# Half-array products for x and logits, decay by diagonal products, and routing steps spread over more iterations, in a three-stage kernel

## Chip, core and metric

One core of a Trainium2 chip runs the whole program. The metric is the device time of one execution in microseconds (us). Five engines work side by side and wait for each other through semaphores: TensorE (PE, matrix products, with its weight loads shown as PEld), VectorE (DVE), ScalarE (ACT), GpSimd (POOL) and SyncE (SP, which here only issues transfers). Each engine takes its instructions in the order of its own queue.

## What is computed

Three stages, each feeding the next, all in float32:

```python
# attention with a decaying state, B=4, H=8, S=768, D=48
for t in range(S):
    cur = einsum('bhd,bhe->bhde', u[None] * kt, vt)
    y[:, :, t] = einsum('bhd,bhde->bhe', rt, state + cur)
    state = w[None, :, :, None] * state + einsum('bhd,bhe->bhde', kt, vt)
x = y.transpose(0, 2, 1, 3).reshape(B * S, H * D)          # 3072 x 384
# mixture of 8 experts, one chosen per token, 384 -> 1024 -> 384
logits = x @ w_gate; e = argmax(logits)
out = softmax(logits)[e] * sigmoid(x @ w_output_gate)[e] * (relu(x @ w1[e]) @ w2[e])
# dense feed-forward, 384 -> 1536 -> 384
result = (silu(out @ w_gate2) * (out @ w_val)) @ w_out
```

## The kernel before, in words

**The attention** takes the 3072 tokens in 24 tiles of 128, six to each of the four sequences. Heads lie in four pairs (q), two of 48 channels padded to 64 in each (j), so that a pair fills the 128 partitions. A loop of 27 iterations (`for i in range(NTILE + 3)`) is written out by hand: inside `tc.manual_schedule`, PE, DVE, ACT and POOL issue in program order. Iteration i holds, in this order, work for several tiles:

- `scaled_r(i+1)`: the tile `rdT` on DVE (L384), and loads of later tiles on SP.
- `bonus(i+1)`: a sum `cb` on DVE (L396) and eight multiplies of the identity into `dsb` on ACT (L400).
- `scores(i)`: 8 products `pss` on PE (L410), each two instructions, with a 64x128 stationary operand; two masked copies into `dsb` on DVE (L414). The two `pss` buffers are the two of the pool `ps_s`.
- the second half of `emit` for tile i-3: a transpose of the logits `lT` on PE (`psl`, L126), and their sum over the four pairs, `lg`, on DVE (L127).
- `state(i-1)`: 8 products `pskv` on PE (L432); at a batch's first tile a copy on DVE (L437), at the following four one multiply-add per pair on DVE (L442), state times decay plus product; at its last tile nothing.
- `scaled_k(i+2)`: `ck`, `kdT` and `kdc` on POOL (L373 to L377).
- `outputs(i-1)`: products `psy` on PE, from the state (L459) and from `dsb` (L466), and the copy `yT` on ACT (L471).
- the first half of `emit` for tile i-2: logits `psl` (L114) and four transposes `psx` (L120) on PE, the copies `lT` (L116) and `xt` (L122) on ACT, and the store of x by SP (L123).

**Routing.** When a batch's last `lg` is there, a generator `route` (and for the first three batches `gate`, for the third also `head_tokens`) is put into the list `routing`. Each call of `advance` takes one step from it, one or two small DVE instructions; the calls stand between the other work of the loop. Before a step on PE the generator yields `TENSOR`; such a step is taken only by `advance(TENSOR)`, and not until two ticks of a counter `now` (three ticks per iteration) have passed since the step before it:

```python
if kind != tensor or kind and since > now[0] - 2:
    return
```

`scores` calls `advance` four times, `state` two to eight times (more from tile HURRY = 18 on), and three calls stand between. The step `psw` (L210) on PE needs the selections made on DVE (L199 to L206).

**Way out of the attention.** `head_tokens` (L495) turns the third batch's routing into row numbers `rows_h`; two gathers on POOL (L1029) fetch tokens for the first expert, `moe.transposed` transposes them on PE (`pt`, L1043) at the start of iteration 24, and `moe.head` begins the first expert's products (`pha`, L1074) after iteration 26, with the fourth batch's routing handed out between its steps.

**PSUM** has eight banks: `ps_m` three (warm-up, `psl`, `pskv`), `ps_s` two, `ps_y` two (`psy`, `psx`), `ps_r` one (routing). From about 150 us on follow the experts, with the third stage's weights converted beside them, and the third stage; they are bound to the order of their own loops.

## Time and profile before

| | us |
|---|---|
| median of 3 runs (856.60 to 857.57) | 857.28 |
| profiled execution, its time | 855.75 |
| its span, first to last instruction | 854.0 |
| PE busy in the span | 820.0 |
| DVE busy | 534.2 |
| ACT busy | 350.9 |
| POOL busy | 215.7 |

Busy time is that in which an engine runs instructions; PE's is modelled at its end, so that a busy PE is not PE at its peak. The granted clock is the share of 2.4 GHz that TensorE was given, with two levels, 1.2 and 2.4 GHz. In a timeline a row merges instructions of one line that follow each other; the time in brackets behind a row is idle time before it and what ended it.

### The profile page before, as it was taken

The page shows a single profiled execution, that of the slowest core. Times are in us where ns is not written, and L with a number is a line of the kernel's source. Part 1 is how long each engine was busy: PE and PEld are TensorE (multiplying, and loading weights), DVE is VectorE, ACT ScalarE, POOL GpSimd, SP SyncE. Part 2 cuts the span into 40 slices and gives each one's busy share as a digit, 9 for nine tenths or more (in the row PEclk, how much of TensorE's full clock was granted, in tenths as well). Part 3 has the DMA queues.
Part 4 walks back from the last instruction along what each step waited for, and adds up shares of the span by engine and source line. Part 5 has one row for each costly group of instructions (what it writes and reads, how often), then busy time and mean ns, then how long its engine had stood idle before and what let it go on. Part 6 is the DMA issues. An engine that isn't in the chain of part 4 may idle for free.

```text
span 854.0 us, 14581 instructions
## 1 busy us (share of the span) xinstructions
PE 820.0 (96%) x5535; PEld 736.6 (86%) x5536; DVE 534.2 (63%) x1097; ACT 350.9 (41%) x793; POOL 215.7 (25%) x206
## 2 busy tenths in 40 slices
PE   7997889999999999999999999999999999999994
PEld 4776677998999989998888888888888888899994
DVE  7889997789999989973555334333533533244532
ACT  3875565474565665663433212221221222122321
POOL 7998672444424422200000100100010010001000
PEclk8999989999999999999999999999999999999997
DMA  8897864665887877442220100100010010001000
GB/s 297 306 329 244 296 232 144 201 184 156 258 252 247 230 254 233 135 147 63 84 84 13 38 0 13 38 1 1 12 38 1 7 38 1 0 8 39 19 1 22
DMA packets 61839, 99.57 MB, mean 117 GB/s; under 512 B 5364, under 2 KB 47872, under 8 KB 61760
## 3 DMA queue, kind: packets, MB, share of 16 engines
q1 hardware_dynamic: 58320, 88.44, 32.0%
q0 software_dynamic: 3440, 10.11, 3.7%
q8 instruction: 45, 0.74, 0.4%
q14 instruction: 34, 0.28, 0.1%
HBM read 82.00 MB, written 16.53 MB: 115 GB/s over the span
## 4 chain that ended last, share of the span: by engine, by line
issue 58%; DVE 16%; POOL 10%; PE 8%; DMA 5%; ACT 1%; SPq 0%; POOLq 0%; DVEq 0%; ACTq 0%
DMA m<-ab 3%; POOL out_dram L1218 2%; POOL kdT L376 2%; DVE w1l L952 2%; POOL kdc L377 2%; DMA yd_all<-in_tr_dram 1%; DVE ab L928 1%; DVE ab L924 1%; DVE dsb L414 1%; POOL ck L373 1%; DVE w2l L952 1%; DVE ab L919 1%; DVE rdT L384 1%; PE pya L1074 1%; DVE h L1094 1%
## 5 line engine op out<-in xcount | busy, mean ns | idle before, releaser
L1242 DVE TENSOR_TENSOR hv<-pg,hv 128x512 f32<-128x512 f32 (+1 forms) x84 | 51.6, 614 | 156.6 <-ACT hv L1241 156.5
L1218 POOL DMA_INDIRECT out_dram<-ot,tokd x24 | 24.8, 1033 | 452.2 <-DVE ot L1217 448.5
L1241 ACT ACTIVATE hv<-pg 128x512 f32<-128x512 f32 (+1 forms) x84 | 45.2, 538 | 169.0 <-PE pg L1237 168.7
L860 ACT CAST hh<-hv 128x512 fp32r<-128x512 f32 (+1 forms) x84 | 47.0, 559 | 141.5 <-DVE hv L1243 141.5
L1211 PE MATMUL po<-wh,hh 128*128 128x384 f32 x288 | 97.1, 337 | 0.0
L1211 PE MATMUL po<-wh,hl 128*128 128x384 f32 x288 | 97.0, 337 | 0.0
L1211 PE MATMUL po<-wl,hh 128*128 128x384 f32 x288 | 97.0, 337 | 0.0
L1074 PE MATMUL ph<-x,w1h 128*128 128x416 f32 x336 | 91.7, 352 | 0.0
L1237 PE MATMUL pg<-xh,wh 128*128 128x512 f32 (+1 forms) x252 | 91.1, 362 | 0.0
L1237 PE MATMUL pg<-xh,wl 128*128 128x512 f32 (+1 forms) x252 | 90.9, 361 | 0.0
L1237 PE MATMUL pv<-xh,wh 128*128 128x512 f32 (+1 forms) x252 | 90.8, 360 | 0.0
L1237 PE MATMUL pv<-xh,wl 128*128 128x512 f32 (+1 forms) x252 | 90.7, 360 | 0.0
L1237 PE MATMUL pv<-xl,wh 128*128 128x512 f32 (+1 forms) x252 | 90.6, 360 | 0.0
L1237 PE MATMUL pg<-xl,wh 128*128 128x512 f32 (+1 forms) x252 | 90.5, 359 | 0.0
L1074 PE MATMUL py<-h,w2h 128*128 128x416 f32 x336 | 90.5, 355 | 0.0
L861 DVE TENSOR_TENSOR hl<-hv,hh 128x512 fp32r<-128x512 f32 (+1 forms) x84 | 51.7, 615 | 45.4 <-ACT hh L860 45.2
L1243 DVE TENSOR_TENSOR hv<-pv,hv 128x512 f32<-128x512 f32 (+1 forms) x84 | 51.6, 615 | 44.0 <-PE pv L1237 43.5
L400 ACT ACTIVATE dsb<-cs,cb 128x128 f32<-128x128 f32 x192 | 58.8, 389 | 37.9 <-DVE cb L396 37.8
L925 POOL TENSOR_TENSOR low<-low,exw 128x384 f32<-128x384 f32 x36 | 40.3, 1119 | 107.7 <-DVE exw L921 82.4
L1074 PEld LDWEIGHTS py<-h,w2h 128*128 128x128 f32 x336 | 63.8, 190 | 0.9
L1074 PEld LDWEIGHTS ph<-x,w1h 128*128 128x128 f32 x336 | 63.4, 189 | 0.5
L1074 PE MATMUL ph<-x,w1l 128*128 128x416 f32 x168 | 60.9, 362 | 2.1 <-DVE h L1094 2.0
(211 smaller groups left out, 1754.4 us busy)
## 6 DMA issues: line engine op xcount, KB each, us to landing
r<-in_w_dram SPq DMA_DIRECT2D x64, 384.0 KB, 4.3
yd_all<-in_tr_dram SPq DMA_DIRECT2D x24, 512.0 KB, 4.7
yd_all<-in_tok_dram SPq DMA_DIRECT2D x24, 384.0 KB, 5.3
m<-ab SPq DMA_DIRECT2D x36, 192.0 KB, 4.2
rw<-m SPq DMA_DIRECT2D x36, 192.0 KB, 2.4
yd_all<-in_tok_dram SPq DMA_DIRECT2D x24, 256.0 KB, 4.2
x_d<-xt SPq DMA_DIRECT2D x24, 192.0 KB, 3.1
cva<-in_w_gate_dram SPq DMA_DIRECT2D x12, 384.0 KB, 3.8
```

The source lines that it names most:

```text
L400: nc.scalar.mul(dsb[:, h, :], ident, cb[:, h : h + 1])
L860: first = nc.scalar.copy(hi, src)
L861: second = nc.vector.tensor_tensor(out=lo, in0=src, in1=hi.bitcast(F32), op=ALU.subtract)
L925: nc.gpsimd.tensor_tensor(out=low, in0=low, in1=ex.bitcast(F32), op=ALU.mult)
L952: nc.vector.tensor_tensor(out=lo, in0=r, in1=hi.bitcast(F32), op=ALU.subtract)
L1074: nc.tensor.matmul(dst[:, 0:n], lhsT=a, rhs=b, start=start and t == 0, stop=stop and t == 2)
L1211: nc.tensor.matmul(po[t], lhsT=a[:, t * P : (t + 1) * P], rhs=bb, start=(f == 0 and j == 0), stop=(f == KF2 - 1 and j == 2))
L1218: st = nc.gpsimd.indirect_dma_start(out=out[:, :], out_offset=bass.IndirectOffsetOnAxis(ap=tokd[:, i : i + 1].bitcast(U32), axis=0), in_=o ...
L1237: nc.tensor.matmul(dst, lhsT=a[:, fs], rhs=bb[:, q, :], start=(q == 0 and j == 0), stop=(q == KD - 1 and j == 2))
L1241: nc.scalar.activation(hv, pg, AF.Sigmoid)
L1242: nc.vector.tensor_tensor(out=hv, in0=pg, in1=hv, op=ALU.mult)
L1243: nc.vector.tensor_tensor(out=hv, in0=pv, in1=hv, op=ALU.mult)
```

## The change

- `emit` makes x and the logits in one set of eight products: for each pair and half, the stationary operand is 64 partitions of `yT`, the moving one a constant `unit` of 64 columns, 48 of the identity and 16 of the gate weights. The result `psx` takes two banks, one per half, of a new pool `ps_x` with one buffer. ACT copies x (`xt`) and the logits (`lh`) out of it; the sum `lg` on DVE then runs over four pairs and two halves from `lh`. `lT`, `psl` and both kinds of transposes go.
- `state` adds the decayed state on PE: eight products of a diagonal tile `dec` (made once, on ACT) with the old state go into `pskv`, and ACT copies the result. The multiply-adds on DVE go.
- `scores` calls `advance` twice instead of four times before iteration 18, `state` twice before tile 18 and eight times after, with all calls behind the products; steps on PE wait four ticks instead of two up to tick 54 (iteration 18).
- `ps_m` has one buffer instead of three. `scores(1)` and two of the head's three accumulators use `ps_x`. `u_tok` moves into the large tile `yd_all`.

Left out below is only the call of `emit` in a branch that these inputs do not take.

```diff
--- before.py
+++ after.py
@@ -107,24 +107,28 @@
     up = sm_t[:, NP : 2 * NP]
     wg = sm_t[:, 2 * NP :].rearrange("p (q g) -> p q g", q=NP)
 
-    def emit(yT, x_rows, lg, pool, ps_m, ps_y):
-
-        psl = ps_m.tile([P, P], F32, name="psl", tag="m")
-        for q in range(NP):
-            nc.tensor.matmul(psl[32 * q : 32 * q + 32, :], lhsT=wg[:, q, :], rhs=yT[:, q, :], start=True, stop=True)
-        lT = pool.tile([P, P], F32, name="lT")
-        nc.scalar.copy(lT, psl)
-
-        psx = ps_y.tile([P, H, 64], F32, name="psx", tag="y")
-        for q in range(NP):
-            nc.tensor.transpose(psx[:, 2 * q : 2 * q + 2, :].rearrange("p h d -> p (h d)"), yT[:, q, :], ident)
-        xt = pool.tile([P, H, D], F32, name="xt")
-        nc.scalar.copy(xt, psx[:, :, 0:D])
-        nc.sync.dma_start(out=x_rows, in_=xt.rearrange("p h d -> p (h d)"))
-        yield
-        psl2 = ps_m.tile([P, NP, 32], F32, name="psl2", tag="m")
-        nc.tensor.transpose(psl2.rearrange("p q e -> p (q e)"), lT, ident)
-        nc.vector.reduce_sum(lg, psl2[:, :, 0:G].rearrange("p q e -> p e q"), axis=AX.X)
+
+    unit = const.tile([P, NP, 64], F32, name="unit")
+    for j in range(2):
+        pr = slice(64 * j, 64 * j + 64)
+        nc.gpsimd.tensor_copy(
+            unit[pr, :, 0:D], ident[pr, 64 * j : 64 * j + D].rearrange("p (o d) -> p o d", o=1).to_broadcast([64, NP, D])
+        )
+    nc.gpsimd.tensor_copy(unit[:, :, D:], wg[:, :, 0:G])
+
+    def emit(yT, x_rows, lg, pool, ps_x):
+
+        psx = ps_x.tile([P, 2, 8, 64], F32, name="psx", tag="x")
+        for q, j in itertools.product(range(NP), range(2)):
+            pr = slice(64 * j, 64 * j + 64)
+            nc.tensor.matmul(psx[:, j, q, :], lhsT=yT[pr, q, :], rhs=unit[pr, q, :], start=True, stop=True)
+        xt = pool.tile([P, NP, 2, D], F32, name="xt")
+        nc.scalar.copy(xt.rearrange("p q j d -> p j q d"), psx[:, :, 0:NP, 0:D])
+        nc.sync.dma_start(out=x_rows, in_=xt.rearrange("p q j d -> p (q j d)"))
+        lh = pool.tile([P, 2, NP, G], F32, name="lh")
+        nc.scalar.copy(lh, psx[:, :, 0:NP, D:])
+        yield
+        nc.vector.reduce_sum(lg, lh.rearrange("p j q e -> p e (j q)"), axis=AX.X)
 
     def route(sl, lg, mx, pool, ps_p, ps_w):
 
@@ -264,7 +268,8 @@
         actx.enter_context(tc.manual_schedule(engines={mybir.EngineType.SP}))
         acst = actx.enter_context(tc.tile_pool(name="acst", bufs=1))
         apool = actx.enter_context(tc.tile_pool(name="apool", bufs=2))
-        ps_m = actx.enter_context(tc.tile_pool(name="ps_m", bufs=3, space=PSUM))
+        ps_m = actx.enter_context(tc.tile_pool(name="ps_m", bufs=1, space=PSUM))
+        ps_x = actx.enter_context(tc.tile_pool(name="ps_x", bufs=1, space=PSUM))
         ps_s = actx.enter_context(tc.tile_pool(name="ps_s", bufs=2, space=PSUM))
         ps_y = actx.enter_context(tc.tile_pool(name="ps_y", bufs=2, space=PSUM))
         ps_r = actx.enter_context(tc.tile_pool(name="ps_r", bufs=1, space=PSUM))
@@ -290,7 +295,7 @@
         def pairs(ap):
             return ap.rearrange("p (q t) -> p q t", q=NP)
 
-        u_tok = acst.tile([P, H, D], F32, name="u_tok")
+        u_tok = carve(H * D).rearrange("p (h d) -> p h d", d=D)
         for i in range(NIO):
             load(i)
             if i == 0:
@@ -329,10 +334,16 @@
             nc.tensor.transpose(pst[:, q, :], we[:, q, :], ident)
         wk_tok = carve(H * D).rearrange("p (h d) -> p h d", d=D)
         nc.scalar.copy(wk_tok, pst.rearrange("p q (j d) -> p (q j) d", j=2)[:, :, 0:D])
+
+        st_b = [acst.tile([P, NP, 64], F32, name=f"st{i}") for i in range(2)]
+
+        dec = carve(NP * 64).rearrange("p (q d) -> p q d", q=NP)
+        for q in range(NP):
+            for j in range(2):
+                pr = slice(64 * j, 64 * j + 64)
+                nc.scalar.mul(dec[pr, q, :], ident[pr, pr], pw[pr, q, P : P + 1])
+        kdc_b = [acst.tile([P, H, 64], F32, name=f"kdc{i}") for i in range(3)]
         nc.gpsimd.memset(yd_all[:, used[0] :], 0.0)
-
-        st_b = [acst.tile([P, NP, 64], F32, name=f"st{i}") for i in range(2)]
-        kdc_b = [acst.tile([P, H, 64], F32, name=f"kdc{i}") for i in range(3)]
         for t in kdc_b:
             nc.gpsimd.memset(t[:, :, D:], 0.0)
         nc.vector.memset(rows_f, 0.0)
@@ -403,8 +414,11 @@
         def scores(i):
             rdT, kdT, kdc, dsb, v_t = S[i]
 
-            banks = [(ps_y, "y"), (ps_m, "m")] if i == 1 else [(ps_s, "s")] * 2
-            pss = [pool.tile([P, NP, P], F32, name=f"pss{j}", tag=tag) for j, (pool, tag) in enumerate(banks)]
+            if i == 1:
+                both = ps_x.tile([P, 2, NP, P], F32, name="pss01", tag="x")
+                pss = [both[:, j] for j in range(2)]
+            else:
+                pss = [ps_s.tile([P, NP, P], F32, name=f"pss{j}", tag="s") for j in range(2)]
             for q, j in itertools.product(range(NP), range(2)):
                 p0 = 64 * j
                 nc.tensor.matmul(
@@ -417,7 +431,8 @@
                     pss[j],
                 )
                 advance()
-                advance()
+                if i >= HURRY:
+                    advance()
 
         def state(i):
             c = i % NCH
@@ -431,21 +446,19 @@
                     p0 = 64 * j
                     nc.tensor.matmul(
                         pskv[p0 : p0 + 64, q, :], lhsT=kdc[:, 2 * q + j, :], rhs=v_t[:, 2 * q + j, :],
-                        start=True, stop=True,
+                        start=(q == 0), stop=(c == 0 and q == NP - 1), skip_group_check=True,
                     )
-            if c == 0:
-                nc.vector.tensor_copy(st_n, pskv)
+            if c > 0:
+                for q in range(NP):
+                    for j in range(2):
+                        pr = slice(64 * j, 64 * j + 64)
+                        nc.tensor.matmul(
+                            pskv[pr, q, :], lhsT=dec[pr, q, :], rhs=st[pr, q, :], start=False, stop=(q == NP - 1),
+                            skip_group_check=True,
+                        )
+            nc.scalar.copy(st_n, pskv)
+            for _ in range(2 if i < HURRY else 2 * NP):
                 advance()
-                advance()
-                return
-            for q in range(NP):
-                nc.vector.scalar_tensor_tensor(
-                    out=st_n[:, q, :], in0=st[:, q, :], scalar=pw[:, q, P : P + 1], in1=pskv[:, q, :],
-                    op0=ALU.mult, op1=ALU.add,
-                )
-                advance()
-                if i >= HURRY:
-                    advance()
 
         def outputs(i):
 
@@ -479,7 +492,7 @@
 
             while routing:
                 g, kind, since = routing[0]
-                if kind != tensor or kind and since > now[0] - 2:
+                if kind != tensor or kind and since > now[0] - (2 if now[0] > 3 * HURRY else 4):
                     return
                 kind = next(g, routing)
                 if kind is not routing:
@@ -503,7 +516,7 @@
                 pool, tag = (const, f"_{g.start}") if late else (apool, "")
                 lgs[g.start] = pool.tile([P, n, G], F32, name="lg" + tag), pool.tile([P, n], F32, name="mx" + tag)
             lg, mx = lgs[g.start]
-            yield from emit(S.pop(i), x_d[i * P : (i + 1) * P, :], lg[:, i - g.start, :], apool, ps_m, ps_y)
+            yield from emit(S.pop(i), x_d[i * P : (i + 1) * P, :], lg[:, i - g.start, :], apool, ps_x)
             if i + 1 == g.stop:
                 routing.append((route(g, lg, mx, apool, ps_r, ps_r), 0, 0))
                 if late:
@@ -562,7 +575,7 @@
                 now[0] += 1
                 advance(TENSOR)
 
-            head = moe.head(ps_m, ps_s)
+            head = moe.head(ps_m, ps_x, ps_s)
 
             def urgent(n, tensor=0):
                 for _ in range(n):
@@ -1045,11 +1058,13 @@
             ends = split(nc, pt[:, :, 0:n], x[:, 0, :, sl], x[:, 1, :, sl])
         return ends
 
-    def head(self, p_y, p_h):
+    def head(self, p_y, p_x, p_h):
 
         env = self.env
         x, _ = self.xs[0]
-        py = [p_y.tile([P, env["CAP"]], F32, name=f"pya{d}", tag="m") for d in range(env["KD"])]
+        py2 = p_x.tile([P, 2, 512], F32, name="pya12", tag="x")
+        py = [p_y.tile([P, env["CAP"]], F32, name="pya0", tag="m"), py2[:, 0, 0 : env["CAP"]], py2[:, 1, 0 : env["CAP"]]]
+        assert len(py) == env["KD"]
         for f in range(env["KF"]):
             ph = p_h.tile([P, env["CAP"]], F32, name="pha", tag="s")
             self.step(0, f, self.ahead[0, f // 2], x, slice(0, HEAD), ph, py)
```

## Rows read from the trace of the kernel before

**Rows 1.** Stretches: us, then busy time and instructions of PE, PEld, DVE, ACT, POOL; granted clock
```profile
30.00:60.00 30.00, 30.00 (x467) 23.81 (x465) 24.42 (x58) 22.50 (x69) 29.53 (x26) 1.00 0.92 318
60.00:90.00 30.00, 25.32 (x339) 20.11 (x335) 29.86 (x64) 18.59 (x57) 25.54 (x24) 0.89 0.77 256
...
350.00:854.00 504.00, 491.99 (x2593) 445.92 (x2592) 221.26 (x383) 140.07 (x268) 29.83 (x29) 0.99 0.10 31
```

**Rows 2.** Timeline, PE, one iteration: start us, us, engine, line, operation, tiles
```profile
36.04 1.16 PE L410 MATMUL pss<-rdT,kdT 64*128 64x128 f32 x16
37.13 0.33 PE L126 MATMUL psl<-cs,lT 128*128 128x128 f32 x1
37.39 0.69 PE L432 MATMUL pskv<-yd_all,kdc 128*64 128x64 f32 x16
38.01 1.09 PE L459 MATMUL psy<-rdT,st 64*64 64x128 f32 x16
...
40.05 0.43 PE L114 MATMUL psl<-yT,sm_t 128*32 128x128 f32 x8
40.41 0.66 PE L120 MATMUL psx<-cs,yT 128*128 128x128 f32 x4
40.99 1.16 PE L410 MATMUL pss<-rdT,kdT 64*128 64x128 f32 x16
```

**Rows 3.** Timeline, DVE, part of an iteration
```profile
56.88 1.37 DVE L414 COPY_PREDICATED dsb<-cs,pss 128x512 f32<-128x512 int32 x2
58.12 0.23 DVE L127 TENSOR_REDUCE lg<-psl 128x16 f32<-128x64 f32 x1
58.25 0.85 DVE L442 SCALAR_TENSOR_TENSOR st<-st,yd_all,pskv 128x64 f32<-128x64 f32 x4
59.01 0.79 DVE L384 TENSOR_TENSOR rdT<-yd_all 128x512 f32<-128x512 f32 x1
...
59.84 0.54 DVE L396 TENSOR_REDUCE cb<-ck 128x8 f32<-128x384 f32 x1
```

**Rows 4.** Timeline, ACT, the eight multiplies of one iteration
```profile
70.04 2.45 ACT L400 ACTIVATE dsb<-cs,cb 128x128 f32<-128x128 f32 x8 [5.27 <-DVE cb L396]
```

**Rows 5.** Costliest lines up to 240 us, ACT: busy us, mean ns, idle before
```profile
L122 ACT COPY xt<-psx 128x384 f32<-128x384 f32 x24 | 11.5, 479 | 2.2 <-ACT lT L116 1.8 <-PE psx L120 0.3
```

**Rows 6.** Timeline, DVE, last batch but one: first and last step of the selections
```profile
134.07 0.17 DVE L192 SCALAR_TENSOR_TENSOR npos<-big,num 128x6 f32<-128x6 f32 x1
...
136.01 0.26 DVE L206 TENSOR_SCALAR sel<-sel,cs 128x192 bf16<-128x192 bf16 x1
```

**Rows 7.** Line 384 up to 150 us: duration in ns, min/median/max
```profile
L384 DVE TENSOR_TENSOR rdT<-yd_all x23: 677/792/1760, 10.9 to 136.2; 128x512 f32<-128x512 f32 x23
```

**Rows 8.** Timeline, PE, around the wait for a selection
```profile
67.88 0.34 PE L210 MATMUL psw<-sel,p_oh 128*128 128x64 bf16 x6 [2.58 <-DVE sel L206]
...
68.91 1.97 PE L459 MATMUL psy<-rdT,st 64*64 64x128 f32 x16
```

**Rows 9.** Stretch behind that wait, columns as in rows 1
```profile
68.90:72.40 3.50, 3.50 (x36) 3.14 (x32) 3.50 (x9) 2.36 (x9) 3.34 (x4) 0.51 0.56 185
```

**Rows 10.** Timeline, DVE, end of the attention
```profile
139.10 0.17 DVE L495 CAST rows_h<-rows_f 128x2 int32<-128x2 f32 x1
...
142.83 0.72 DVE L414 COPY_PREDICATED dsb<-cs,pss 128x512 f32<-128x512 int32 x1
```

**Rows 11.** Timeline, POOL, second gather of the head's tokens
```profile
141.02 0.96 POOL L1029 DMA_INDIRECT xg<-x_d,rows_h  x1 [0.30 <-issue]
```

**Rows 12.** Tile xg up to 152 us: from issue to landing
```profile
DMA to landing us min/median/max: 3.3/3.4/3.5
```

**Rows 13.** Timeline, PE, end of the attention
```profile
140.36 1.16 PE L410 MATMUL pss<-rdT,kdT 64*128 64x128 f32 x16
...
145.22 0.82 PE L1043 MATMUL pt<-cs,xg 128*128 128x128 f32 x6
...
150.05 0.37 PE L1074 MATMUL pha<-x,w1l 128*128 128x256 f32 x1
```

More of the change, by code (lines that the diff above doesn't have):

```diff
@@ L721, in sequential @@
                 for _ in emit(
-                    yT, x_d[bass.ds(i * P, P), :], lg[:, bass.ds(i, 1), :].rearrange("p o g -> p (o g)"), sq, ps_m, ps_y
+                    yT, x_d[bass.ds(i * P, P), :], lg[:, bass.ds(i, 1), :].rearrange("p o g -> p (o g)"), sq, ps_y
                 ):
```

## The prediction, made before the changed kernel ran

> **What bounds the kernel now.** I read the table of stretches first, then one iteration on TensorE (PE) and one on VectorE (DVE), then the waits, last the way out of the attention. From 350 us on PE works 492 of 504 us [rows 1]: what the attention gains or loses moves the end by as much, and only the attention, up to 150 us, is edited. It has two halves. From 30 to 60 us PE is busy 30.00 of 30 us and GpSimd (POOL) 29.53, while DVE has 5.6 us to spare [rows 1]. One iteration on PE lasts from one `pss` to the next, 4.95 us, with no gap [rows 2]. From 60 us on DVE is busy 29.86 of 30 us and PE has 4.7 us idle [rows 1]: the routing of a finished batch has been put between DVE's copies. So up to about 50 us a cheaper PE or POOL would be felt, and afterwards a shorter DVE queue.
>
> **PE, term by term.** Out of an iteration go `psl` (40.05 to 40.41, 0.36 us), the transposes `psx` (to 40.99, 0.58) and the second `psl` (37.13 to 37.39, 0.26): 1.2 us [rows 2]. In come eight half-array products in 16 instructions, a stationary operand of 64x128 and 64 moving columns. The nearest row from above is `pss`, same stationary operand and 128 moving columns: 1.09 for 16. From below it is `pskv`, 64 stationary and 64 moving columns: 0.62 for 16 [rows 2]. Both are equally near; I take the middle, 0.85.
>
> The Trainium skill ("TensorE: Matmul & The Clock Gate", section on LDWEIGHTS) prices a weight load by its columns, at 1.2 of them per ns, which for 128 is 107 ns. Sixteen in single file would be an estimated 1.7 us by that page, and the iteration 0.85 us longer than by my middle. The trace differs: `pss`, with 16 loads of this very form, takes 1.09 [rows 2].
>
> The decay by diagonal products adds another 16 instructions of 64x64 with 64 columns in the 16 iterations that have both a former state and a next one. `pskv` is the nearest row: 0.6 (at most `psy`, 64x64 with 128 columns, 1.02 [rows 2]). An ordinary iteration becomes 4.95 - 1.2 + 0.85 + 0.6 = 5.2 us; one without decay loses 0.35. Four of the first kind and two of the second make +0.3 per batch. Before 50 us I put +0.3 (from -1.5 to +1.5 by the bounds), as POOL keeps its pace beside it.
>
> **DVE, from the score copies of iteration 8 to those of iteration 22 (52 to 138.6 us), where it sets the pace.** The step to iteration 23 goes by either engine, about 5 us in both schedules, and is left at 0.
> - Removed: the state's four multiply-adds, 0.76 us as their starts show (58.25 to 59.01 [rows 3]), in ten of these iterations, and two plain copies at a batch's start, taken at half of that: -8.4. Their replacement, a copy on ScalarE (ACT), lies beside 2.45 us of `dsb` and the other copies [rows 4], in an iteration of 5.2; `xt` keeps its 0.48 [rows 5], and `lh` replaces `lT` of equal size.
> - Pushed past the end: I counted the calls of `advance` in both schedules. At the score copies of iteration 22 the old one has finished group 2's selections; in the new one positions, one-hot and selections still lie ahead. Those run from 134.07 to 136.27 [rows 6], less two multiply-adds of 0.19: -1.8.
> - Added: `lg` sums 128 values instead of 64. The two reductions of [rows 3] differ by 320 values and 0.31 us, so 0.07 each, 14 times: +1.0.
> - Added wait: `ex` of groups 0 and 1 now comes right behind `bonus`, so its exponentials on ACT stand behind eight `dsb` multiplies, 2.45 us [rows 4]. The next step on DVE wants them after a copy and a step, about 1.4 us. Waiting 0 to 1.1 us, twice; POOL runs undisturbed meanwhile, so I take half: +1.2. Behind it in DVE's queue is the second score copy.
> - Lost to evenness: between score pairs 9 to 10 and 10 to 11 DVE now has only 3.15 and 3.75 us of work: copies 1.24, `lg` 0.13, `rdT` 0.72 and `cb` 0.5 make 2.6 [rows 3], waits beside POOL some 0.35, and one step (0.2) and three (0.8) of the routing are left there by the new count. PE takes 5.2. It cannot copy scores that are not there. 2.05 + 1.45, less 0.5 that it lags on arrival: +3.0.
>
> Sum -5.0. How long a step takes beside POOL is the unsure part: `rdT` alone takes 677 to 1760 ns [rows 7], and I keep today's durations for the steps. Waiting 0.2 us more or less on each of some 40 steps is 4 us either way at the most (half is likely).
>
> The old schedule also makes PE wait 2.58 us for a selection, after which the same 16 products take 1.97 instead of 1.09 us [rows 2, 8] and the granted clock stands at 0.51 of 2.4 GHz, the 1.2 GHz level [rows 9]. The new distance of four ticks ends this wait. I count nothing for it, because DVE had work all through [rows 1].
>
> **The way out.** One iteration later is also where `rows_h` of group 2 now falls: in iteration 23 instead of 22. Behind it hangs the gather of the head's tokens, and behind that `pt`, which stands in PE's queue ahead of the last `psy`. Today `rows_h` starts at 139.10, the second gather at 141.02, landing 3.4 us later, 144.4 [rows 10 to 12]; PE comes to `pt` at 145.22 and does not wait [rows 13]. Afterwards, from the start of `pss` in iteration 23: `pss` 1.09, two score copies 1.35, `lg` and two sums 0.55: `rows_h` at 3.0, and 5.3 later, as today, landed at 8.3. PE gets to `pt` after 1.09 + 0.2 + 0.6 + 0.6 + 2.04 + 0.85 = 5.4, so it waits 2.9 (more, if DVE comes later to the scores; less, if PE does). Then half a `pt` 0.3, `psy` 2.04, `psx` 0.85, a wait of about 1.0, and `psx` again 0.85: the head starts at 13.4. The 1.0 is the single `psx` buffer: `xt` 0.48 and a shorter `lh` [rows 5] must have read it, and the last two tiles follow each other directly. Today that distance is 150.05 - 140.36 = 9.69 [rows 13]. It begins 0.75 us earlier against DVE, whose second copy now ends at 143.55 [rows 10], 3.2 after `pss` starts, instead of 2.45. So 10.95 instead of 6.5 after DVE's finish: +4.4.
>
> Setup adds eight small ACT multiplies and three POOL copies while both still wait for loads; taken as 0 (at most +1 if the loads do not cover them).
>
> **Sum.** +0.3 - 5.0 + 4.4 = -0.3. The profiled execution took 855.75 us (span 854.0 and 1.75 around it), 1.53 below the median of 857.28; it would become 855.45, and the median 857.0.
>
> **Rivals.**
> 1. *The relief arrives in full.* The stretch of [rows 9], 3.5 us at half rate, costs PE 1.75 us, and there is one behind the `psw` wait of each of the two groups. If both lie on the path after all, 3.5 us more are saved: -3.8, 853.5 (850 to 855.5). For: the granted clock is only 0.89 from 60 to 90 us [rows 1], and behind each such stretch PE has lost its lead over DVE. Against: DVE's 29.86 of 30, which leaves no time in which it waited for PE.
> 2. *The late gather decides, slower.* It is hidden only if `rows_h` starts within 0.1 us of `pss` in iteration 23; I have 3.0. A wait of 2.58 was enough for the lower clock level [rows 8, 9]; with one of 2.9 and the same fall, two `psy` groups take 0.88 us longer each, 1.9 with `psx`, and DVE 0.75 behind, as today, adds to the wait: -0.3 + 1.9 + 0.75 = +2.35: 859.6 (to 862). For: the place is certain. Against: the wait may be split in two by the first gather, and the clock need not fall.
> 3. *The half-array products are no cheaper than `pss`*, so the change doesn't make x and logits cheap: 1.09 instead of 0.85 in every iteration where PE is the bound, about 12: +2.9 - 0.3 = +2.6: 859.9. Against: half the moving columns.
>
> **Chances.** Forecast 0.45 (own range 854.5 to 859), rival 1 0.30, rival 2 0.20, rival 3 0.05. A measurement of this kernel can tell about 0.2%, 1.7 us, from no change. Of the forecast 0.08 lies faster than that, 0.30 within, 0.07 slower; rival 1 is faster; of rivals 2 and 3 0.04 lie within, 0.21 beyond. Faster 0.38, same 0.34, slower 0.28. The range 851.5 to 861 leaves out the lower quarter of rival 1 and the upper third of rivals 2 and 3, some 0.16 in all.
>
> **What would show it.** Right: no multiply-adds on DVE; `psx` of 16 instructions in 0.6 to 1.1 us; no idle time before `psw`; `pss` of iteration 23 four to five us earlier than 140.36; an idle stretch of two to four us before `pt`; a head start within 2 us of 150.05. Wrong: DVE still full at 29.9 of 30 with longer steps; no wait before `pt`; PE idle shrinking without the span following.

## Result and the profile after

The changed kernel took 864.39 us (median of 4 runs, 863.64 to 867.55), the kernel before beside it on the same chip 856.94. The ratio is 1.0107, interval 1.0087 to 1.0127: 7 us slower by the medians, about 9 by the ratio, and outside the range of the prediction. The profiled execution took 863.64 us (span 861.8) against 855.75 (854.0) before, 7.9 more. Comparisons of times below go by ratios to the kernel before, timed beside it on the same chip.

The page of the profile shows the intended shift, less DVE and more PE (before: PE 820.0, DVE 534.2):

```profile
span 861.8 us, 15191 instructions
PE 828.5 (96%) x5863; PEld 752.7 (87%) x5864; DVE 524.7 (61%) x1029; ACT 358.8 (42%) x821; POOL 216.8 (25%) x209
```

Where the time went is read from the starts of `pss` on PE, one per iteration, and of the head's first product `pha`: iteration 10 starts at 61.28 us (59.18 before), iteration 23 at 143.08 (140.36, [rows 13]), `pha` at 159.51 (150.05). So there are three pieces: **+2.1 before iteration 10, +0.6 from 10 to 23, +6.7 on the way out**, together +9.5 at `pha`. From `pha` to the end the profiled execution takes 704.1 us after the change and 705.7 before; 1.6 come back there, from a cause that stays open.

**The start.** Timeline of PE, then of ACT, before iteration 2 is done:

```profile
13.49 0.66 PE L334 MATMUL pst<-cs,we 128*128 128x128 f32 x4
16.92 0.54 PE L355 MATMUL psk<-wok,ones 128*128 128x4 f32 x2 [2.77 <-ACT yd_all L336]
19.62 1.12 PE L447 MATMUL pskv<-yd_all,kdc 128*64 128x64 f32 x16 [2.17 <-POOL kdc L388]
20.50 1.95 PE L479 MATMUL psy<-dsb,yd_all 128*64 128x128 f32 x16
22.38 1.84 PE L424 MATMUL pss<-rdT,kdT 64*128 64x128 f32 x16
```

```profile
4.91 1.28 ACT L344 ACT_TABLE_LOAD   x1 [4.77 <-DMA cs<-in_cst_dram]
6.21 2.85 ACT L344 ACTIVATE yd_all<-cs,yd_all 64x64 f32<-64x64 f32 x8
9.08 1.28 ACT L331 ACTIVATE we<-yd_all 128x128 f32<-128x128 f32 x4
11.72 4.79 ACT L411 ACTIVATE dsb<-cs,cb 128x128 f32<-128x128 f32 x16 [1.36 <-DVE cb L407]
16.41 0.46 ACT L336 COPY yd_all<-pst 128x384 f32<-128x384 f32 x1
```

The set-up is not in the hand-written order. `pst`, the transposes for `wk_tok`, and its copy on ACT ran early before:

```profile
6.94 0.38 PE L329 MATMUL pst<-cs,we 128*128 128x128 f32 x2
8.44 0.48 ACT L331 COPY yd_all<-pst 128x384 f32<-128x384 f32 x1 [0.42 <-PE pst L329]
```

Now `pst` stands behind the scores of tile 1, at 13.49, and its copy runs at 16.41, behind sixteen `dsb` multiplies. `psk` on PE and `kdc` on POOL wait for it, `pskv` for `kdc`. Two suspects are in these rows: the eight `dec` multiplies (L344), now first in ACT's queue, and the single bank left to `ps_m`, which warm-up, `pst`, `psk` and `pskv` have to share.

**One iteration on PE**, the same columns; it answers to [rows 2]:

```profile
38.45 1.11 PE L424 MATMUL pss<-rdT,kdT 64*128 64x128 f32 x16
39.49 0.69 PE L447 MATMUL pskv<-yd_all,kdc 128*64 128x64 f32 x16
40.10 0.68 PE L455 MATMUL pskv<-st,yd_all 64*64 64x64 f32 x16
40.62 1.04 PE L472 MATMUL psy<-rdT,st 64*64 64x128 f32 x16
41.59 1.09 PE L479 MATMUL psy<-dsb,yd_all 128*64 128x128 f32 x16
42.62 1.11 PE L124 MATMUL psx<-unit,yT 64*128 64x64 f32 x16
43.56 1.11 PE L424 MATMUL pss<-rdT,kdT 64*128 64x128 f32 x16
```

From start to start the 16 instructions of `psx` take 0.94 us, the diagonal products (L455) 0.52, the iteration 5.11 (4.95 before).

**The loop from iteration 10 to 23**: stretches of both kernels, columns as in [rows 1], first of the kernel before, then after, and DVE's waits from iteration 9 to 23 after the change:

```profile
59.18:140.36 81.18, 70.34 (x974) 55.87 (x970) 80.29 (x192) 51.28 (x156) 56.95 (x51) 0.92 0.75 252
```

```profile
61.28:143.08 81.80, 73.48 (x1158) 64.74 (x1157) 76.67 (x152) 53.63 (x166) 59.63 (x50) 0.90 0.75 252
```

```profile
DVE eo L235 <- ACT eo L232: 3.0, 2, 1.6
DVE rk L182 <- PE psp L176: 0.9, 2, 0.7
DVE dsb L428 <- PE pss L424: 0.8, 2, 0.4
```

DVE works 3.6 us less (76.67 for 80.29) and stands idle 4.2 us more (5.1 for 0.9). What it works less came back as idle time, 4.7 us of it in waits by name, and the stretch is 0.6 longer. PE waits for DVE as long as before. Its waits for a DVE result in the two stretches (us in all, times, longest), before and then after, and the longest one after:

```profile
PE psw L210 <- DVE sel L206: 5.7, 3, 2.6
PE pss L410 <- DVE dsb L414: 2.8, 3, 1.1
```

```profile
PE pss L424 <- DVE dsb L428: 6.1, 5, 3.2
PE psw L214 <- DVE sel L210: 2.2, 1, 2.2
```

```profile
79.47 2.59 PE L424 MATMUL pss<-rdT,kdT 64*128 64x128 f32 x16 [3.18 <-DVE dsb L428]
```

The wait before `psw` is gone for group 0 (not for group 1, 2.15 us), but in its place `pss` waits for the score copies: 8.3 us in all for 8.5, and behind the longest the products run at the 1.2 GHz level again (granted clock 0.50 from 79.47 to 83.00).

**The way out**, PE from `pss` of iteration 23 on, and the cast of `rows_h` on DVE:

```profile
143.08 1.11 PE L424 MATMUL pss<-rdT,kdT 64*128 64x128 f32 x16
...
147.53 1.11 PE L124 MATMUL psx<-unit,yT 64*128 64x64 f32 x16
150.16 0.88 PE L1056 MATMUL pt<-cs,xg 128*128 128x128 f32 x3 [1.52 <-DMA xg<-x_d,rows_h]
151.65 0.88 PE L1056 MATMUL pt<-cs,xg 128*128 128x128 f32 x3 [0.62 <-DMA xg<-x_d,rows_h]
152.45 1.97 PE L472 MATMUL psy<-rdT,st 64*64 64x128 f32 x16
154.35 1.97 PE L479 MATMUL psy<-dsb,yd_all 128*64 128x128 f32 x16
156.25 1.43 PE L124 MATMUL psx<-unit,yT 64*128 64x64 f32 x16
158.47 1.11 PE L124 MATMUL psx<-unit,yT 64*128 64x64 f32 x16 [0.79 <-ACT lh L129]
159.51 0.39 PE L1089 MATMUL pha<-x,w1l 128*128 128x256 f32 x1
```

```profile
146.24 0.17 DVE L508 CAST rows_h<-rows_f 128x2 int32<-128x2 f32 x1
```

`rows_h` falls into iteration 23, `pt` waits for both gathers (1.52 and 0.62), and the two `psy` groups behind it take 1.97 us instead of 1.04 and 1.09: the granted clock of the stretch from 152.45 to 156.25 is 0.50, the 1.2 GHz level. It is 0.50 already in the first `pt` group (150.16 to 151.04), and 1.00 in the `psx` ahead of the wait.

### The profile page after: what moved, and what is told of

Its sections match the earlier page's. It is cut to its first block, busy times and chain, and to the rows that moved or that the text cites. A ratio compares the mean times of both kernels' runs of the same rounds, so it can differ in the third digit from the quotient of the medians.

```text
span 861.8 us, 15191 instructions
## 1 busy us (share of the span) xinstructions
PE 828.5 (96%) x5863; PEld 752.7 (87%) x5864; DVE 524.7 (61%) x1029; ACT 358.8 (42%) x821; POOL 216.8 (25%) x209
## 4 chain that ended last, share of the span: by engine, by line
issue 57%; DVE 12%; POOL 4%; PE 4%; DMA 3%; ACT 1%; SPq 0%; POOLq 0%; DVEq 0%; ACTq 0%
DMA m<-ab 3%; POOL out_dram L1233 2%; DVE w1l L965 2%; DVE ab L941 2%; DVE ab L937 1%; DVE w2l L965 1%; DVE h L1109 1%; DVE ab L932 1%; PE pya L1089 1%; DVE low L940 1%; POOL xg L1042 1%; DVE exw L934 1%; PE pha L1089 1%; POOL low L938 1%; DVE x L874 1%
```

## Experiments

Twelve kernels, 6 to 12 executions of each. The kernel before had medians of 854.74 us beside e1 to e4, 855.22 beside e5 to e8 and 855.66 beside e9 to e12, up to 2.5 below the one that the expectations count from, so that medians are read with their ratios. Starts are of `pss` in the named iteration of the one profiled execution, in us; "way out" is from `pss` of iteration 23 to the first `pha`. Starts vary: e11 and e12 have the same code up to the last tile, and iteration 10 begins at 59.10 and 57.76 (the stretch from 10 to 23 is 81.9 and 81.8).

| kernel | it. 2 | it. 10 | it. 23 | 10 to 23 | way out | median | ratio to before, interval |
|---|---|---|---|---|---|---|---|
| before | 19.70 | 59.18 | 140.36 | 81.2 | 9.7 | | 1 |
| after | 22.38 | 61.28 | 143.08 | 81.8 | 16.4 | 864.39 | 1.0107 (1.0087 to 1.0127) |
| e1 `dec` later | 23.87 | 63.46 | 145.60 | 82.1 | 17.8 | 866.60 | 1.0121 (1.0093 to 1.0149) |
| e2 old hand-out | 22.74 | 61.35 | 141.52 | 80.2 | 11.0 | 857.62 | 1.0026 (1.0010 to 1.0042) |
| e3 hand-out alone | 19.19 | 59.10 | 139.82 | 80.7 | 15.8 | 860.02 | 1.0055 (1.0033 to 1.0076) |
| e4 decay alone | 19.59 | 64.91 | 144.88 | 80.0 | 10.2 | 859.79 | 1.0034 (1.0014 to 1.0054) |
| e5 e2, other banks | 19.45 | 63.84 | 143.93 | 80.1 | 11.3 | 858.99 | 1.0033 (1.0021 to 1.0045) |
| e6 x, logits alone | 21.57 | 60.87 | 143.22 | 82.4 | 11.1 | 859.23 | 1.0032 (1.0020 to 1.0044) |
| e7 decay on two engines | 19.38 | 57.56 | 139.28 | 81.7 | 11.0 | 855.90 | 1.0006 (0.9993 to 1.0018) |
| e8 e7, four ticks | 19.87 | 57.88 | 141.20 | 83.3 | 11.0 | 857.84 | 1.0022 (1.0010 to 1.0035) |
| e9 after, two ticks | 22.06 | 62.00 | 144.98 | 83.0 | 11.1 | 859.99 | 1.0051 (1.0038 to 1.0063) |
| e10 before, late diagonals | 19.30 | 59.13 | 140.01 | 80.9 | 10.2 | 854.47 | 0.9991 (0.9979 to 1.0003) |
| e11 e7, `lh` in order | 19.81 | 59.10 | 141.00 | 81.9 | 11.1 | 856.34 | 1.0005 (0.9993 to 1.0018) |
| e12 e11, last tile apart | 19.59 | 57.76 | 139.57 | 81.8 | 10.0 | 853.56 | 0.9980 (0.9968 to 0.9991) |

**e1.** The `dec` multiplies are issued behind iteration 0, the rest as changed.

```diff
-                nc.scalar.mul(dec[pr, q, :], ident[pr, pr], pw[pr, q, P : P + 1])
...
                 weights(i, 0)
+                if i == 0:
+                    for q in range(NP):
+                        for j in range(2):
+                            pr = slice(64 * j, 64 * j + 64)
+                            nc.scalar.mul(dec[pr, q, :], ident[pr, pr], pw[pr, q, P : P + 1])
```

> The changed kernel, with the eight multiplies that make `dec` on ScalarE put behind iteration 0 instead of ahead of the setup's other ScalarE work. Theory A (three separate losses: about +2.1 us at the start from these multiplies, no gain in the loop, +6.7 on the way out from the late `rows_h` of group 2): `pss` of iteration 10 comes back to 59.2 to 59.8 us (changed kernel 61.28, before 59.18), and the time falls by about 2, to 862.4. Theory B (the start is swallowed, as the loop goes by VectorE from 60 us on): `pss` of iteration 10 comes earlier, but that of iteration 23 does not (143.1), and the time stays at 864.4 within 0.7.

Neither theory's numbers came: the ratio is that of the change (intervals overlap), and the start is later, not earlier. The multiplies left the head of ACT's queue, and `pst` still ran at 13.73; now they stand ahead of the copy that PE waits for. PE's row, then ACT's:

```profile
20.04 0.59 PE L351 MATMUL psk<-wok,ones 128*128 128x4 f32 x2 [5.66 <-ACT yd_all L336]
```

```profile
16.65 2.83 ACT L575 ACTIVATE yd_all<-cs,yd_all 64x64 f32<-64x64 f32 x8
19.51 0.48 ACT L336 COPY yd_all<-pst 128x384 f32<-128x384 f32 x1
```

So the place of `dec` at the head of ACT's queue is not what delays the start. B's other half, that the loop swallows a late start, is not borne out either: 2.2 us later at iteration 10 were still 2.5 at iteration 23.

**e2 and e3.** The hand-out alone, undone in the changed kernel (e2), or put into the kernel before (e3, the same counts of calls and the same ticks the other way, its calls in `state` still between the multiply-adds). The edit of e2:

```diff
                 advance()
-                if i >= HURRY:
-                    advance()
+                advance()
...
-            for _ in range(2 if i < HURRY else 2 * NP):
+            for _ in range(2 if c == 0 else NP if i < HURRY else 2 * NP):
...
-                if kind != tensor or kind and since > now[0] - (2 if now[0] > 3 * HURRY else 4):
+                if kind != tensor or kind and since > now[0] - 2:
```

> The changed kernel, with the hand-out of routing steps as it was before (two per score copy, two or NP behind a state, distance of two ticks). Theory A (late `rows_h` of group 2 costs the way out): `rows_h` in iteration 22 again, no idle time before `pt`, the way from `pss` of iteration 23 to the first `pha` 10.5 to 12 instead of 16.4 us, and 4 to 6 us off: 858.4 to 860.4, still slower than before by the start's 2.1. Theory C (the half-array products and diagonal products on TensorE are the loss, the hand-out is not): the waits before `psw` come back, iteration 23 starts later than 143.1, and the time is 863 or more.

> The kernel before, with the new hand-out alone (old x and logits, multiply-adds on VectorE). Theory A: `rows_h` of group 2 goes to iteration 23 and `pt` waits; from `pss` of iteration 23 to `pha` 13 to 15 instead of 9.7 us; VectorE stays full in the loop, so that iteration 23 starts 0 to 2 us earlier than 140.4 at the most: 859 to 862. Theory C (the hand-out is harmless or a gain, as it takes the 2.6 us wait before `psw` away): 854 to 857.

Theory A both times by the way out (e2's time by its ratio; its median lies 0.8 us below A's range). Without the new hand-out the way out is 11.0 us and the kernel 0.8% faster than the change; with nothing else, the kernel before loses 0.55%, and the way out is the only piece that is longer. PE in e3:

```profile
146.74 0.52 PE L1045 MATMUL pt<-cs,xg 128*128 128x128 f32 x3 [1.73 <-DMA xg<-x_d,rows_h]
148.61 0.87 PE L1045 MATMUL pt<-cs,xg 128*128 128x128 f32 x3 [1.35 <-DMA xg<-x_d,rows_h]
...
149.63 1.97 PE L461 MATMUL psy<-rdT,st 64*64 64x128 f32 x16
```

The same wait and the same half clock, without any half-array product in the kernel.

**e4 and e6.** The diagonal products alone on the kernel before (`state` and `dec` as in the change), and the half-array products alone (`emit` and its banks as in the change; `state` and the hand-out as before).

> The kernel before, with the diagonal products for the state's decay alone (the ScalarE copy with them, `dec` made at the same place as in the change; old x and logits, old hand-out). Theory A: +2.1 us at the start; VectorE loses 0.76 us of work in ten iterations, of which 3 to 6 us come off between iterations 9 and 22; `rows_h` in iteration 22: 853 to 856. Theory C (the products on TensorE and the copy on ScalarE cost as much as they take off VectorE, even where VectorE sets the pace): iteration 23 no earlier than 140.4 plus the start's 2.1, 858 to 861.

> The half-array products for x and logits alone, with their banks (one for `ps_m`) and the old hand-out; the state's decay by multiply-adds on VectorE, no `dec`. Theory A: the start is late here too, `pss` of iteration 2 at 22 to 24, although ScalarE has no `dec` to make; then an iteration of 4.6 us on TensorE instead of 4.95 (0.94 for the products in place of 1.2), or 4.8 to 4.95 if POOL sets the pace; with VectorE as full as before from 60 us on, iteration 23 starts between 140 and 142: 856 to 858. Theory C (the products cost as much as what they replace): iteration 5.0 or more, iteration 23 after 143, 859 or more.

Both came out at C's figures, for other reasons than C's. In e4 the start and PE cost more than A's 2.1 us (iteration 10 at +5.7, an iteration of 5.42 on PE), and the loop behind it gave back 1.2 us, not 3 to 6. Iteration 2 was on time there, at 19.59, with `dec` at the head of ACT's queue but three banks in `ps_m`. In e6 the iteration on PE did fall, to 4.65 (35.92 to 40.57), though the start was late without any `dec`; besides the start, 1.4 us were lost on the way out and 1.2 in the loop from 10 to 23, 82.4 us, with DVE nearly as full as before (81.6 us busy) and the sum `lg` dearer on it (355 ns instead of 206).

**e5.** e2 with `dec` late as in e1, and `pst` and `psk` in the banks of `psy`.

```diff
-        pst = ps_m.tile([P, NP, P], F32, name="pst", tag="m")
+        pst = ps_y.tile([P, NP, P], F32, name="pst", tag="y")
...
-        psk = ps_m.tile([P, NP], F32, name="psk", tag="m")
+        psk = ps_y.tile([P, NP], F32, name="psk", tag="y")
```

> The changed kernel with the old hand-out of e2, the `dec` multiplies behind iteration 0 as in e1, and `pst` and `psk` in the two banks of `psy` instead of the single bank that `ps_m` has left. Theory A (the start is late because warm-up, `pst`, `psk` and `pskv` now take turns in one bank, so that `wk_tok` and with it `kdc` come late): `pss` of iteration 2 at 19.5 to 20.2 us (22.74 in e2, 23.87 in e1, 19.70 before), and 2 to 3 us off e2's 857.6: 854.6 to 855.6. Theory D (the start goes by POOL or by loads; the bank only shifts who waits): iteration 2 stays at 22 or later, 857 to 858.

A's place is right: iteration 2 is back at 19.45. Its price is not: behind the first wait there is now a second. ACT and then PE:

```profile
21.02 2.45 ACT L407 ACTIVATE dsb<-cs,cb 128x128 f32<-128x128 f32 x8 [1.09 <-DVE cb L403]
23.38 0.35 ACT L454 COPY st<-pskv 128x256 f32<-128x256 f32 x1
```

```profile
19.45 2.08 PE L420 MATMUL pss<-rdT,kdT 64*128 64x128 f32 x16 [2.33 <-DVE rdT L391]
23.78 1.12 PE L442 MATMUL pskv<-yd_all,kdc 128*64 128x64 f32 x16 [2.25 <-ACT st L454]
...
25.74 1.92 PE L467 MATMUL psy<-rdT,st 64*64 64x128 f32 x16
```

The state's copy, moved to ACT, stands behind eight `dsb` multiplies; `pskv` of tile 1 needs both that copy's bank and its result and waits 2.25. The products run at half rate from `pss` at 19.45 on, behind an earlier wait of 2.33, and still do after the second. Iteration 3 starts at 30.42 (25.19 before). In the change itself this copy holds up nothing there: `pskv` at 24.15 follows `pss` without a gap.

**e7.** e5 with the old multiply-adds on DVE up to tile 8 and the diagonal products from tile 9 on.

```diff
-            if c > 0:
+            if c > 0 and i >= DIAG:
...
-            nc.scalar.copy(st_n, pskv)
+            if i < DIAG and c > 0:
+                for q in range(NP):
+                    nc.vector.scalar_tensor_tensor(
+                        out=st_n[:, q, :], in0=st[:, q, :], scalar=pw[:, q, P : P + 1], in1=pskv[:, q, :],
+                        op0=ALU.mult, op1=ALU.add,
+                    )
+            elif i < DIAG:
+                nc.vector.tensor_copy(st_n, pskv)
+            else:
+                nc.scalar.copy(st_n, pskv)
...
+DIAG = 9
```

> As e5, and the decay by multiply-adds on VectorE up to iteration 8 (where TensorE and POOL set the pace), by diagonal products from iteration 9 on (where VectorE does). Theory A (the diagonal products cost 0.5 us each where TensorE is the bound and give back where VectorE is): `pss` of iteration 10 at 55.5 to 57.5 (61.35 in e2), iteration 23 two to three us ahead of e5's: 852 to 853.5, below the kernel before. Theory D (POOL's 4.9 us per iteration hold it there, or the lead is lost where VectorE sets the pace from 60 us on): within 0.7 of e5.

Iteration 3 starts at 26.48, iteration 10 is 6.3 us ahead of e5 and 1.6 ahead of the kernel before. Of the 6.3, 4.7 are left at iteration 23 and 3.1 in the medians; the time is that of the kernel before. Neither theory's time came: 855.90 is 3.1 below e5 (D: within 0.7) and above A's 852 to 853.5. A is right on where the products cost, and part of the lead was lost, as D says.

**e8.** The text on record says that the diagonal products run throughout; the kernel that ran had the multiply-adds of e7 up to tile 8, so it is e7 with one line changed, and is compared with e7.

```diff
-                if kind != tensor or kind and since > now[0] - 2:
+                if kind != tensor or kind and since > now[0] - (2 if now[0] > 3 * HURRY else 4):
```

> As e5, with the change's distance of four ticks between a selection and its product on TensorE up to tick 54, the rest of the old hand-out kept. (Decay by diagonal products throughout.) Theory A (the wait before `psw`, 3.0 us in e2, and the half clock behind it cost time once VectorE has work taken off it): no wait before `psw` of group 0, `rows_h` still in iteration 22, 1 to 3 us below e5: 852 to 854. Theory E (VectorE is behind anyway and only catches up in that wait, so its end moves nothing): within 0.7 of e5.

The 3.4 us wait before `psw` of group 0 in e7 is gone, and iteration 12 starts at 69.08 instead of 74.31. By iteration 23 that lead has turned into a lag of 1.9, and the kernel is no faster than e7 (1.0022 and 1.0006, with intervals that overlap). Theory E: taking that wait away gained nothing. As in the change, waits of `pss` for the score copies took its place: 5.8 us from iteration 10 to 23, 2.8 in e7, while those before `psw` fell from 6.2 to 2.9.

**e9.** The change with the tick distance alone undone (the last line of the diff of e2).

> The changed kernel with one line undone: the distance between a selection and its product on TensorE is two ticks again from the first iteration on; the spreading of the steps stays. Theory A (the way out costs what it does because `rows_h` of group 2 comes after the scores of iteration 23): counted out, `rows_h` goes back to iteration 22, `pt` does not wait, `pss` of 23 to the first `pha` takes 10.5 to 12 instead of 16.4 us; the start stays late (iteration 2 at 22 or later): 857.5 to 860. Theory F (the spreading itself delays it, the ticks do not): `rows_h` stays behind the scores of iteration 23 and the time at 863 or more.

A: `rows_h` at 143.50, ahead of iteration 23 (144.98), no wait before `pt`, way out 11.1 (11.05). One line of the change makes the late gather.

**e10.** The kernel before with e7's division of the decay.

> The kernel before with diagonal products from iteration 9 on only, `dec` made behind iteration 0; up to iteration 8 the old multiply-adds on VectorE. Theory A (e4's loss was the start, where the state's copy waits behind `dsb` on ScalarE, and 0.5 us per iteration where TensorE sets the pace): start as before (iteration 3 at 25.2 to 26.5, iteration 10 at 59 to 60), loop from 10 to 23 in 80.0 instead of 81.2 as in e4, way out as before: 853 to 854.5. Theory G (the loop's gain of 1.2 in e4 was only the late start being caught up): iteration 23 at 140 to 141, 855 to 856.5.

Start and way out are close to those of the kernel before, as A says, and the time cannot be told from it (the median, 854.47, falls into A's range, 1.2 below the kernel before). The loop gained 0.3 us (80.9) instead of 1.2, which is nearer to G. In e5 and e7, whose code is the same from iteration 10 on, it is also the loop that begins later that is shorter (80.1 from 63.84, 81.7 from 57.56): it looks as if part of e4's gain was a late start caught up, which single profiles do not show for certain.

**e11 and e12.** First the sum `lg` on data in order; then also, for the last tile alone, `apart`: one half of the products in a bank of `ps_y`, the other in that of `ps_m`, each with its own copies.

```diff
-        lh = pool.tile([P, 2, NP, G], F32, name="lh")
-        nc.scalar.copy(lh, psx[:, :, 0:NP, D:])
+        lh = pool.tile([P, G, 2, NP], F32, name="lh")
+        nc.scalar.copy(lh.rearrange("p e j q -> p j q e"), psx[:, :, 0:NP, D:])
...
+        if apart:
+            halves = [p.tile([P, NP, 64], F32, name=f"psx{j}", tag=tag) for j, (p, tag) in enumerate(apart)]
```

> As e7, with `lh` written with the eight partial sums of an expert side by side, so that VectorE's sum over them reads in order. Theory A (VectorE sets the pace from 60 us on, and the sum of 128 values with a stride takes 353 ns where 64 took 209): the sum takes 250 to 280 ns, 1.0 to 1.4 us less in 14 of them, and the time 854.5 to 855.2 against e7's 855.9. Theory E (what is taken off VectorE comes back as waits): within 0.5 of e7.

> As e11, with the two halves of the last tile's products in a bank of `ps_y` and the bank of `ps_m` instead of `ps_x`, so that they need not wait for the copies of the tile before. Theory A (the single buffer costs 0.8 us of waiting on the way out): no wait before the second `psx`, `pss` of 23 to the first `pha` 10.0 to 10.3 instead of 11.0 us, 0.7 to 1.0 below e11: 853.6 to 854.4. Theory H (the head then waits for its own first transfers or buffers): the same as e11 within 0.3.

The sum fell from 353 to 271 ns, as A of e11 says, and the loop took 81.9 us for 81.7: E. Line 131 of e7, then of e11 (ns, min/median/max):

```profile
L131 DVE TENSOR_REDUCE lg<-lh x17: 336/353/369, 46.9 to 142.1; 128x16 f32<-128x128 f32 x17
```

```profile
L131 DVE TENSOR_REDUCE lg<-lh x17: 261/271/283, 48.4 to 143.8; 128x16 f32<-128x128 f32 x17
```

On the way out e12 does what A says. PE runs both sets of `psx` without a gap, and the head starts 10.0 us after iteration 23:

```profile
147.63 2.00 PE L129 MATMUL psx<-unit,yT 64*128 64x64 f32 x32
149.56 0.38 PE L1111 MATMUL pha<-x,w1l 128*128 128x256 f32 x1
```

e12 is below both kernels: 0.9980 of the one before (0.9968 to 0.9991), some 2 us. Against e11 it is 2.8 us faster in the medians, where A put 0.7 to 1.0 and the way out is 1.1 shorter; the rest is not explained.

## Why the prediction was wrong

**Products on PE: right.** 0.94 for `psx` where 0.85 was taken between 0.62 and 1.09, 0.52 for the decay (0.6), 5.11 for the iteration (5.2). Rival 3 is out. By the column price that the Trainium skill gives for weight loads ("TensorE: Matmul & The Clock Gate", section on LDWEIGHTS), sixteen loads of 128 columns in single file would take an estimated 1.7 us; the trace has 0.94 with the loads in it.

**"Setup ... taken as 0 (at most +1 if the loads do not cover them)": failed, +2.1 by iteration 10.** I costed the multiplies and copies that were added and not the two buffers that `ps_m` lost. e6 has the delay without any `dec`, e4 has `dec` early and three banks and no delay at iteration 2, and e5 has iteration 2 on time again with other banks for `pst` and `psk` (and `dec` late): the banks are the cause. e5 and e4 show a second cost that the change itself does not reach: the state's copy behind `dsb` on ACT, after which iteration 3 starts 5.2 and 4.3 us later than before. e7, with the multiply-adds left on DVE there, has most of both removed (iteration 3 at 26.48): of the step "a copy on ACT lies beside 2.45 us of `dsb`" the word beside was wrong there, where `pskv` waits for it.

**"-5.0 on DVE", from the score copies of iteration 8 to those of iteration 22: failed, +0.2.** The same stretch in both kernels, from the end of the second copy of iteration 8 to that of iteration 22, columns as in [rows 1], before and then after:

```profile
51.75:138.58 86.83, 75.99 (x1065) 60.46 (x1063) 86.35 (x206) 53.54 (x163) 63.42 (x56) 0.92 0.78 267
```

```profile
53.94:140.93 86.99, 78.67 (x1257) 69.40 (x1251) 81.80 (x159) 56.89 (x178) 66.81 (x57) 0.90 0.79 267
```

Of the sum, the terms of work came to -9.2 (-8.4, -1.8 and +1.0) and those of waiting to +4.2 (1.2 and 3.0). DVE's idle time grew by 4.7, from 0.5 to 5.2, so waiting was nearly right in all, though not in its parts: `eo` waited 1.35 and 1.63 us for ACT, 3.0 where I took 1.2 (`ex` was handed out as predicted, with the score copy behind it held up), and some 1.7 were left for evenness, put at 3.0. **The work is the term that failed: it fell by 4.6, not by 9.2.** The multiply-adds and copies did go. But the sum `lg` took 354 ns instead of 206, +0.15 each where I took +0.07, 1.9 us in all for 1.0; the 14 `rdT` took 2.5 us more in all, and six conversions of weights 0.6. The routing steps that stayed changed one by one, by up to 1.8 us, but hardly in sum. Some 0.6 us are not assigned. "Today's durations", kept by the forecast and called its unsure part, are a premise that did not hold for `rdT` in this execution.

Nor is DVE's work alone what sets the loop's length. From iteration 10 to 23 DVE was busy between 74.8 us (e4) and 81.6 (e6), with 76.6 in e9, and these three took 80.0, 82.4 and 83.0 us; the two kernels and the twelve experiments took between 80.0 and 83.3, whatever was removed: some 7 us of multiply-adds and copies (e2: -1.0), `lg` made shorter (e11: +0.2 on e7), the `psw` wait (e8: +1.6 on e7). DVE's 29.9 of 30 [rows 1] was read as a bound. The rows fit a ring better, in which scores, copies and selections wait for each other and a wait that is taken away comes back at the next place, as PE's 8.5 and 8.3 us do. That is argued from the waits: which of them binds in each iteration was not taken apart further. Rival 1, the relief in full, is out by the same rows: the half-rate stretches moved with the waits, and the granted clock of the loop is 0.90 for 0.92.

On the durations: `rdT` from iteration 10 to 23 took 1085 ns in the mean before and 1188 after; but e11 and e12, with the same code in the loop, have 911 and 1122, so a tenth more is within what one profile differs from another. The Trainium skill ("SBUF — State Buffer", the section on two separate sides) has VectorE and GpSimd share a port pair, held for a whole instruction, when VectorE reads two operands from SBUF and GpSimd reads SBUF too. The spread of [rows 7], 677 to 1760 ns for one form, agrees with it; no run here took GpSimd's work away to show it alone.

**The way out: right in its place, short in its size.** `rows_h` came 3.2 us behind `pss` of iteration 23 (predicted 3.0), PE was at `pt` after 5.6 (5.4), waited 2.1 (2.9), and the single buffer cost 0.8 (1.0). Predicted 13.4, measured 16.4: of the missing 3 us, 1.8 are both `psy` groups at half rate, 0.8 the two `psx`, 0.6 the waits with `pt` at half rate between and behind them, less 0.2 at the single buffer. The step that failed is that the forecast's sum has the clock stay up behind the wait. That was rival 2, though not the whole of it: its 0.75 for DVE lagging as today did not come (DVE's second copy ended 2.6 us after `pss` of iteration 23, the forecast's 2.45). e3 and e9 show the cause, the hand-out in e3 and within it the four ticks in e9. I gave rival 2 0.20 because the wait might be split by the first gather; it was, and the clock fell in both e3 and the change.

Counted from `pss` to `pss`, as in the table, the forecast's three pieces are +0.3, -4.3 (the -5.0, less the 0.75 that iteration 23 begins earlier against DVE) and +3.7 (13.4 for 9.7). Measured are +2.1, +0.6 and +6.7, and 1.6 back behind `pha`. Rival 2 had the way out nearly right; that its upper bound, 862, lies near the measured time is luck, since it took the start and the loop from the forecast.

## What to carry to other kernels

Count a change's buffers like its instructions: a pool cut from three banks to one, or a copy moved to a queue where long work stands ahead of it, can make the start late, and nothing in the steady state tells of it. Work taken off an engine that is busy 99% of a stretch is worth only what its neighbours leave free; ask for each microsecond removed which wait takes it, and whether the work that stays keeps its durations. When steps are handed out later, follow the last of them to the first transfer that hangs on it, and price the clock behind the wait as well.

## What the runs showed of the hardware

Waits of 2 us or less on PE were followed by the 1.2 GHz level: 1.52 us ahead of the first `pt` group, with a granted clock of 1.00 before it and 0.50 behind it, and 0.62 ahead of the second gave `psy` 1.97 instead of 1.04 to 1.09 us. In e9 and e12, where PE did not wait there, the same products stood at 1.09. The length of one wait did not settle it: in e3 the clock was still 1.00 behind a wait of 1.73 us and 0.50 behind the next, of 1.35; the `pss` of iteration 2 had 0.50 behind 2.33 us in e5 and 1.00 behind 2.35 in e7.

What half-array products cost depended on the stationary operand. With one of 64x128, 16 instructions took 0.94 us with 64 moving columns and 1.04 with 128 (`pss`, 38.45 to 39.49): halving the columns took off a tenth. With one of 64x64 they took 0.52 (L455) and 0.97 (`psy` L472, 40.62 to 41.59): there it took off nearly half.
